# Q and K cast head by head in attention, and the DMA queue's order

## The chip, the cores and the metric

One core of a Trainium2 chip runs the whole program. The metric is the device time of one execution in microseconds (us). The kernel before took 928.75, 928.95 and 930.42 in three runs; the median is 928.95.

## The reference

Attention over 4 batches of 8 heads (576 positions, 64 wide), a mixture of experts with a capacity, and a dense layer behind it:

```
scores = q @ k.T / sqrt(D)                       # causal
cum    = cumsum(max(s, 0))
bias   = min(-(cum[:, None] - cum[None, :]), 0)
attn   = softmax(where(causal, -1e9, scores + bias)) @ v
x      = experts(attn)                           # token choice by gate, capacity N // E
out    = max(x @ w_in, 0) ** 2 @ w_out
```

The change touches the attention part and the conversion of w_out that runs beside it. Both kernels compute all of this.

## The kernel before

TensorE multiplies in fp32r, so each operand that must keep its precision is split: a rounded part (a cast to fp32r) and the rest (a subtraction). For a pair of heads the tiles are `Q1`, `K1`, `Q2` and `K2`. The raw loads `q2` and `k2` hold Q and K twice, in partitions 0 to 63 and 64 to 127. K1 is the cast of both copies of K; Q1 has the cast of Q in its lower half and Q's rest in its upper half; K2 holds K's rest and Q2 the cast of Q. One matmul of Q1 with K1 and one of Q2 with K2 (L205, L206) add up to the full product. Q2's 64 rows are copied from Q1 by a DMA (L174), and rows 64 to 67 of Q2 and K2 carry the bias: ones, and two rows from the cumulative sum that DMAs bring (L148, L149).

`attention` walks over 160 tiles, called steps here: 16 pairs of heads, ten steps a pair, five to a head. The five tiles of a head are its blocks of query rows, from the last (576 columns of scores) to the first (64). At a step, `scores` puts the matmuls of its tile on TensorE; `softmax` (L222, VectorE) takes the row maximum; then come the functions that the table `slot` holds for this step; `transposes` turns the tile of two steps before (L250, TensorE); `expo` (L233) is the exponent on ScalarE; and `flush` copies transposed tiles out of PSUM (L240 on VectorE, L238 on ScalarE). Values times weights (`av`, L276) run for the pair before, and `av_out` copies the result into oT.

The engines work through their instructions in the order in which the program issues them, so these tables set what stands behind what. `PR` and `P1` say at which step of a pair `prep` of the next pair is called: bias rows, K's cast (L162) and K's subtraction on GpSimd (L165) at step 2, Q's cast (L173), the DMA of Q2 and Q's subtraction (L175) at step 3, each over both heads (1152 columns). `load_pair` of the pair after next is called at the first step of a pair, ahead of its scores. `CS` places the conversion of w_out, one block of 512 columns a pair, sixteen in all: `load` (a DMA of 512 KB into r, L837) at step 2, `begin` at step 7 (ex on GpSimd, L850, and the first sg on VectorE, L874), `begin2` at step 8 (the second sg), `end` at step 9 (woutR, L885). In the first pair each comes five steps later (`C0`). What is not converted in attention is converted later, beside the experts, by `conv.step`.

All these DMAs are issued by SyncE, in order. Eight of its issues can be under way: an issue waits until the one eight before it has landed.

Of the kernel before, what the change touches and what calls it, by code (L numbers as in the profile page):

```python
# [7 lines left out]
FR = mybir.dt.float32r  # L8
# [3 lines left out]
AF = mybir.ActivationFunctionType  # L12
OP = mybir.AluOpType
# [3 lines left out]
B, H, S, D = 4, 8, 576, 64  # L17
# [5 lines left out]

XA = [1, 0]
LQ = 3
QP = 0
G2 = [(1, 5), (0, 1)]
G2L = [(3, 5), (0, 3)]
XB = 1
# [6 lines left out]
def f32(ap):  # L36
    return ap.bitcast(FT)
# [28 lines left out]
def attention(tc, cn, qT, kT, vm, vt, s, wg, xd, L):  # L66
    nc = tc.nc
    NP = B * H // 2
# [13 lines left out]
    wk = pool("a_wk", 2)  # L82
# [6 lines left out]
    RAW = {}  # L89
# [46 lines left out]
    nc.vector.tensor_sub(brow[:, 1, :], sr, f32(brow[:, 0, :]))  # L136
    PREP = {}

    def prep(p, u):
        if u == 0:  # L140
            q2, k2 = RAW[p]
            Q1 = wk.tile([128, 2, S], FR, name="Q1")
            K1 = wk.tile([128, 2, S], FR, name="K1")
            Q2, K2 = Q2S[p % 2], K2S[p % 2]
            PREP[p] = (Q1, K1, Q2, K2, q2)
            for a in range(2):
                hd = 2 * p + a
                nc.sync.dma_start(f32(K2[66:68, a, :]), f32(brow[hd:hd + 1]))  # L148
                nc.sync.dma_start(f32(Q2[64:66, a, :]), f32(brow[hd:hd + 1]))  # L149
            if p == 0:  # L150
                for a in range(2):
                    nc.scalar.activation(Q1[:, a], q2[:, a], AF.Copy)
                    nc.scalar.activation(Q2[0:64, a], q2[0:64, a], AF.Copy)
                    nc.vector.tensor_copy(K1[:, a], k2[:, a])
                    (nc.gpsimd if a else nc.vector).tensor_tensor(K2[0:64, a], k2[0:64, a], f32(K1[0:64, a]),
                                                                  op=OP.subtract)
                    nc.vector.tensor_tensor(Q1[64:128, a], q2[64:128, a], f32(Q1[64:128, a]), op=OP.subtract)  # L157
                return
            if QP:
                nc.gpsimd.tensor_tensor(Q1, q2, zero[:, :, None].to_broadcast([128, 2, S]), op=OP.add)  # L160
            if QP < 2:
                nc.vector.tensor_copy(K1, k2)  # L162
            else:
                nc.gpsimd.tensor_tensor(K1, k2, zero[:, :, None].to_broadcast([128, 2, S]), op=OP.add)
            nc.gpsimd.tensor_tensor(K2[0:64], k2[0:64], f32(K1[0:64]), op=OP.subtract)  # L165
        else:
            RAW.pop(p)
            if p == 0:
                ones(1)
                return  # L170
            Q1, K1, Q2, K2, qs = PREP[p]
            if not QP:
                nc.vector.tensor_copy(Q1, qs)  # L173
            nc.sync.dma_start(f32(Q2[0:64]), f32(Q1[0:64]))  # L174
            nc.gpsimd.tensor_tensor(Q1[64:128], qs[64:128], f32(Q1[64:128]), op=OP.subtract)  # L175


    E = [fx.tile([128, 128 * (i + 1)], FT, name=f"e{i}") for i in range(5)]
# [9 lines left out]
    tiles = [(hd, i) for hd in range(B * H) for i in (4, 3, 2, 1, 0)]  # L188

    def scores(hd, i):  # L190
        Q1, K1, Q2, K2 = PREP[hd // 2][:4]
        a = hd % 2
        n = max(256, NN[i])
        c0 = I0S[i]
        if i == 4:
            t = ps.tile([128, 2, 512], FT, name="sc4")
            parts = [(t[:, 0, :288], 0, 288), (t[:, 1, :288], 288, 576)]
            v = t[:, :, :288]
        else:
            t = ps.tile([128, 512], FT, name="sc", bufs=SCB)  # L200
            parts = [(t[:, :n], 0, n)]
            v = t[:IM[i], :NN[i]]
        for o, x0, x1 in parts:
            m = x0 <= c0 < x1
            nc.tensor.matmul(o, Q1[:, a, c0:c0 + 128], K1[:, a, x0:x1], start=True, stop=False)  # L205
            nc.tensor.matmul(o, Q2[:, a, c0:c0 + 128], K2[:, a, x0:x1], start=False, stop=not m)  # L206
            if m:
                nc.tensor.matmul(o[:, c0 - x0:c0 - x0 + IM[i]], cn.identb, cn.tri[:, :IM[i]], start=False, stop=True)  # L208
        SC[hd, i] = v
# [158 lines left out]
                f, a = jobs.popleft()  # L368
                f(*a)

    prep(0, 0)
    load_pair(1)
    load_v(0)

# [2 lines left out]
    for g in range(2):  # L377
        nc.sync.dma_start(wbd[64 * g:64 * g + 64, :, 8 * g:8 * g + 8],
                          bass.AP(tensor=wg.tensor, offset=wg.offset + g * 512, ap=[[8, 64], [1024, 4], [1, 8]]))
    prep(0, 1)  # L380
    slot = {}

    def at(t, f, *a):
        slot.setdefault(t, []).append((f, a))
# [1 line left out]
    NT = len(tiles)  # L386
    AVS = [0, 0, 4, 5, 5, 8, 8]
    ORD = 2
    P1 = 3
    C0 = 5  # L390
    LS_ = [2, 2, -1, -1, -1, -1, 0]
    LO_ = [3, 2]
    LT = 3
    GB = [12, 4]
    PTB = 3
    CS = [2, 7, 8, 9]
    PR = [2, 3]
    AVO = [1, 8]
    for p in range(NP):
        t0 = 10 * (p + 1) + LA  # L400
        last = p == NP - 1
        avs, avo = (LS_, LO_) if last else (AVS, AVO)
        for n in range(7):
            at(t0 + avs[n], av, p, n)
        at(t0 + avo[0], av_out, p, 0)
        at(t0 + avo[1], av_out, p, 1)
        if p + 1 < NP:
            at(10 * p + PR[0], prep, p + 1, 0)
            at(10 * p + (PR[1] if p else P1), prep, p + 1, 1)
        for f, n in zip((cn.conv.load, cn.conv.begin, cn.conv.begin2, cn.conv.end), CS):  # L410
            at(max(0, 10 * p + n + (0 if p else C0)), f, *([True] if f == cn.conv.begin else []))
# [14 lines left out]
    for t in range(tend):  # L426
        if t < NT:
            hd, i = tiles[t]
            if hd % 2 == 0 and i == 4:
                p = hd // 2  # L430
                if p + 2 < NP:
                    load_pair(p + 2)
# [381 lines left out]
class Convert:  # L814


    def __init__(self, tc, cn, win, wout):
        self.nc, self.cn = tc.nc, cn
        self.loaded = self.begun = self.done = 0
        self.hold = False  # L820
        self.two = set()
# [18 lines left out]
    def begin(self, pool=False):  # L840
        n = self.begun
        if n >= self.loaded:
            return
        self.begun += 1
        hw = self.r64[n][:, :, :, 1]
        ex = self.cn.cv.tile([128, 4, 128], FT, name="ex", bufs=3)
        sg = self.cn.cv.tile([128, 4, 128], I32, name="sg", bufs=1)

        if pool:
            self.nc.gpsimd.tensor_tensor(ex, hw.bitcast(FT), self.cn.m112[:, :, None].to_broadcast([128, 4, 128]),  # L850
                                         op=OP.mult)
        else:
            self.nc.scalar.activation(ex, hw.bitcast(FT), AF.Copy, scale=2.0 ** -112)
        if n < NB2:
            self.half(n, sg, 0, 13, OP.logical_shift_right)
        else:

            u = self.r64[n].rearrange("p c f w -> p (c f w)").bitcast(U16).rearrange("p (f w) -> p f w", w=4)
            o = sg.rearrange("p c f -> p (c f)").bitcast(U16).rearrange("p (f w) -> p f w", w=2)
            self.nc.scalar.activation(o[:, :, 0], u[:, :, 1], AF.Identity, bias=self.cn.mhalf, scale=2.0 ** -13)  # L860
        self.ex[n] = (ex, sg)

    def begin2(self):
        n = self.begun - 1
# [575 lines left out]
```

## Time and profile before

| what | us |
|---|---|
| median of three runs | 928.95 |
| the profiled execution | 930.37 |
| its span in the profile | 928.60 |
| TensorE busy | 879.3 (95%) |
| VectorE busy | 583.9 (63%) |
| ScalarE busy | 465.8 (50%) |
| GpSimd busy | 274.9 (30%) |

A profile is of one execution. Its times run from the start of the span. PE is TensorE, DVE VectorE, ACT ScalarE, POOL GpSimd and SP SyncE (SPq its queue). A number with L is a line of the kernel. Busy shares are over the whole span, while attention ends at about 223 us and the rest belongs to routing, experts and the dense layer; what a change in attention is worth is read from the rows of that stretch. Ends of matmuls are modelled, so starts are the safer reading.

### The profile page before, as it was taken

To read this page: it belongs to the slowest core of one execution; us is meant where nothing else is said; L and a number is where in the kernel's file an instruction comes from. 1 tells how busy PE (TensorE), PEld (TensorE's weight loads), DVE (VectorE), ACT (ScalarE), POOL (GpSimd) and SP (SyncE) were. 2 spreads that over 40 slices of the span, in tenths; PEclk is the share of its full clock that TensorE was granted. 3 is DMA by queue.
4 is the path that set the end of the run, shared out by engine and by line. 5 is a ranking of instruction groups with operands and counts; after the bars stand their busy time and mean duration, and the time that the engine had idled before them with its cause. 6 is when DMAs were issued, how large, how long until landed. Compare 5 with 4: busy or idle time off the path is not lost.

```text
span 928.6 us, 17302 instructions
## 1 busy us (share of the span) xinstructions
PE 879.3 (95%) x6200; PEld 736.5 (79%) x6200; DVE 583.9 (63%) x1565; ACT 465.8 (50%) x1092; POOL 274.9 (30%) x231
## 2 busy tenths in 40 slices
PE   4999999998788899999999999999999999999996
PEld 3676767766588877888998887989788899898885
DVE  7788988886787779847766556666633444442222
ACT  6677767776334666533543323453333454544332
POOL 4454554550103454625001000300100444523233
PEclk9999999999599999999999999999999999999998
DMA  6977597751635632304531100643100350140001
GB/s 168 226 192 188 141 245 190 189 150 46 203 96 156 198 103 88 91 1 142 165 104 37 33 1 12 212 125 96 35 1 1 93 168 1 53 119 1 0 1 46
DMA packets 73975, 95.60 MB, mean 103 GB/s; under 512 B 8128, under 2 KB 53184, under 8 KB 73888
## 3 DMA queue, kind: packets, MB, share of 16 engines
q1 hardware_dynamic: 68560, 79.93, 31.6%
q0 software_dynamic: 3360, 11.01, 3.7%
q10 hardware_dynamic: 1968, 3.54, 1.1%
q8 instruction: 49, 0.80, 0.3%
q14 instruction: 38, 0.31, 0.1%
HBM read 80.31 MB, written 9.44 MB: 97 GB/s over the span
## 4 chain that ended last, share of the span: by engine, by line
PE 79%; DVE 10%; DMA 4%; issue 3%; ACT 2%; POOL 1%; SPq 1%; DVEq 0%; ACTq 0%; POOLq 0%
PE h L1064 10%; PE h L1065 10%; PE h L1066 10%; PE acc L1112 7%; PE acc L1113 7%; PE acc L1114 7%; PE av L276 5%; PE pt L250 5%; PE acc L1064 3%; PE acc L1065 3%; PE acc L1066 3%; DVE Q L173 2%; DMA raw<-in_w 2%; PE sc L205 2%; PE sc L206 2%
## 5 line engine op out<-in xcount | busy, mean ns | idle before, releaser
L1174 ACT ACTIVATE s<-h 128x512 f32<-128x512 f32 (+1 forms) x80 | 44.4, 555 | 202.1 <-PE h L1066 173.2
L1178 DVE TENSOR_TENSOR s<-s 128x512 f32<-128x512 f32 (+1 forms) x80 | 51.1, 639 | 140.0 <-ACT sH L1177 139.9
L1064 PE MATMUL h<-yH,winH 128*128 128x512 f32 (+1 forms) x332 | 123.0, 371 | 0.7 <-ACT yH L1158 0.7
L1065 PE MATMUL h<-yL,winH 128*128 128x512 f32 (+1 forms) x332 | 120.6, 363 | 0.1
L1066 PE MATMUL h<-yH,winL 128*128 128x512 f32 (+1 forms) x332 | 120.3, 362 | 0.0
L1112 PE MATMUL acc<-wH,sH 128*128 128x512 f32 x288 | 114.8, 399 | 0.0
L989 ACT ACTIVATE wH<-raw 128x512 fp32r<-128x512 f32 x128 | 79.8, 628 | 68.5 <-DMA raw<-in_w 38.9
L1113 PE MATMUL acc<-wL,sH 128*128 128x512 f32 x288 | 112.4, 390 | 0.0
L1114 PE MATMUL acc<-wH,sL 128*128 128x512 f32 x288 | 112.4, 390 | 0.0
L233 ACT ACTIVATE e<-sc,nm 128x576 f32<-128x576 f32 (+4 forms) x160 | 84.0, 525 | 48.1 <-DVE junk L222 41.7
L1179 POOL TENSOR_TENSOR sL<-s,sH 128x512 fp32r<-128x512 f32 (+1 forms) x48 | 67.4, 1405 | 132.8 <-DVE s L1178 132.8
L992 DVE TENSOR_TENSOR wL<-raw,wH 128x512 fp32r<-128x512 f32 x104 | 74.6, 722 | 46.6 <-ACT wH L989 42.7
L222 DVE TENSOR_SCALAR_CACHE_REDUCE junk<-sc 128x576 bf16<-128x576 f32 (+4 forms) x160 | 77.7, 485 | 30.9 <-PE sc L208 20.5
L250 PE MATMUL pt<-ident,e 128*128 128x128 f32 x448 | 82.1, 289 | 7.5 <-ACT e L233 6.1
L205 PE MATMUL sc<-K,Q 128*128 128x288 f32 (+2 forms) x192 | 72.8, 384 | 10.4 <-DVE Q L157 10.4
L1064 PE MATMUL h<-xH,wH 128*128 128x288 f32 x256 | 78.5, 307 | 2.4 <-DVE hL L1142 2.0
L1064 PE MATMUL acc<-hH,wH 128*128 128x288 f32 x256 | 78.1, 305 | 1.7 <-ACT wH L989 1.7
L1066 PE MATMUL h<-xH,wL 128*128 128x288 f32 x256 | 76.0, 297 | 2.0 <-POOL wL L992 1.4
L1066 PE MATMUL acc<-hH,wL 128*128 128x288 f32 x256 | 76.1, 297 | 0.1
L1065 PE MATMUL h<-xL,wH 128*128 128x288 f32 x256 | 76.2, 297 | 0.0
L1065 PE MATMUL acc<-hL,wH 128*128 128x288 f32 x256 | 76.0, 297 | 0.0
L250 PEld LDWEIGHTS pt<-ident,e 128*128 128x128 f32 x448 | 49.4, 144 | 29.1 <-ACT e L233 19.1
(218 smaller groups left out, 2057.6 us busy)
## 6 DMA issues: line engine op xcount, KB each, us to landing
raw<-in_w SPq DMA_DIRECT2D x128, 256.0 KB
k<-in_kT SPq DMA_DIRECT2D x30, 288.0 KB
q<-in_qT SPq DMA_DIRECT2D x30, 288.0 KB
r<-in_wout SPq DMA_DIRECT2D x16, 512.0 KB
r<-in_win SPq DMA_DIRECT2D x16, 512.0 KB
vb<-in_vm SPq DMA_DIRECT2D x16, 256.0 KB
Q<-Q SPq DMA_DIRECT2D x8, 288.0 KB
QB<-Q SPq DMA_DIRECT2D x7, 288.0 KB
```

Source lines behind the costliest of these rows:

```text
L205: nc.tensor.matmul(o, Q1[:, a, c0:c0 + 128], K1[:, a, x0:x1], start=True, stop=False)
L222: nc.vector.tensor_scalar(o, v, -0.125, None, op0=OP.mult, op1=OP.min, accum_out=nm[:m])
L233: nc.scalar.activation(o, v, AF.Exp, bias=nm[:m], scale=0.125, accum_out=sums[b % 2][:m, i, hd % H:hd % H + 1])
L250: nc.tensor.transpose(pt[:, j, :], (E4[hd % 2] if i == 4 else E[i])[:, 128 * j:128 * j + 128], cn.ident)
L989: S.activation(hi, src, AF.Copy)
L992: (G if eng[1] == "G" else V).tensor_tensor(lo, src, f32(hi), op=OP.subtract)
L1064: T.matmul(o, wh, xh, start=first, stop=False)
L1065: T.matmul(o, wh, xl, start=False, stop=False)
L1066: T.matmul(o, wl, xh, start=False, stop=last)
L1112: T.matmul(o, hi[:, c0:c0 + 128], wh, start=f == 0, stop=False)
L1113: T.matmul(o, hi[:, c0:c0 + 128], wl, start=False, stop=False)
L1114: T.matmul(o, lo[:, c0:c0 + 128], wh, start=False, stop=f == NB2 - 1)
```

## The change

`prep` now works on one head, in two calls. The first casts Q's head (576 columns) on VectorE and issues the DMA of its Q2 rows; the second casts K's head on VectorE and puts both subtractions on GpSimd. Both calls of a head fall on one step: 4 for the first head and 9 for the second (in the first pair 5 and 9). A new function `bias` issues the bias rows, at step 1. `load_pair` of the pair after next moves from the start of the pair to step 5. The conversion of w_out gets a third part, `begin1`, with the first sg; `load` moves to step 9, `begin` stays at 7, `begin1` is at 8, `begin2` and `end` at 12 and 13, which is steps 2 and 3 of the next pair.

```diff
+    def bias(hd):
+        p, a = hd // 2, hd % 2
+        for t in (K2S[p % 2][66:68], Q2S[p % 2][64:66]):
+            nc.sync.dma_start(f32(t[:, a]), f32(brow[hd:hd + 1]))
...
-            nc.vector.tensor_copy(K1, k2)
-            nc.gpsimd.tensor_tensor(K2[0:64], k2[0:64], f32(K1[0:64]), op=OP.subtract)
+            nc.vector.tensor_copy(Q1, q)
+            nc.sync.dma_start(f32(Q2[0:64]), f32(Q1[0:64]))
         else:
-            nc.vector.tensor_copy(Q1, qs)
-            nc.sync.dma_start(f32(Q2[0:64]), f32(Q1[0:64]))
-            nc.gpsimd.tensor_tensor(Q1[64:128], qs[64:128], f32(Q1[64:128]), op=OP.subtract)
+            nc.vector.tensor_copy(K1, k)
+            nc.gpsimd.tensor_tensor(K2[0:64], k[0:64], f32(K1[0:64]), op=OP.subtract)
+            nc.gpsimd.tensor_tensor(Q1[64:128], q[64:128], f32(Q1[64:128]), op=OP.subtract)
...
-    P1 = 3
-    C0 = 5
+    CS0 = [7, 12, 13, 14, 15]
-    CS = [2, 7, 8, 9]
-    PR = [2, 3]
+    CS = [9, 7, 8, 12, 13]
+    PR = [4, 4, 9, 9]
+    PR0 = [5, 5, 9, 9]
...
+            for a in range(2):
+                at(10 * p + 1, bias, 2 * p + 2 + a)
+                for u in range(2):
+                    at(10 * p + (PR if p else PR0)[2 * a + u], prep, 2 * p + 2 + a, u)
+        if p + 2 < NP:
+            at(10 * p + 5, load_pair, p + 2)
...
+    def begin1(self):
+        n = self.begun - 1
+        if 0 <= n < NB2 and n not in self.one:
+            self.one.add(n)
+            self.half(n, self.ex[n][1], 0, 13, OP.logical_shift_right)
```

On TensorE the order of the instructions is the same in both kernels. On VectorE, in an even-numbered pair and the start of the next one, it was this (junk is the softmax, sg and woutR the conversion, eT and oT copies out of PSUM):

```order
L874 TENSOR_SCALAR sg<-r_616 128x512
L222 TENSOR_SCALAR junk,nm<-sc 64x64
L885 SCALAR_TENSOR_TENSOR woutR<-ex,sg 128x512
...
L222 TENSOR_SCALAR junk,nm<-sc 128x320
L162 CAST K_782<-k_562 128x1152
L222 TENSOR_SCALAR junk,nm<-sc 128x192
L240 COPY oT<-av 128x256
L173 CAST Q_781<-q_561 128x1152
L222 TENSOR_SCALAR junk,nm<-sc 64x64
```

and now it is this, from the end of one pair's second head on:

```order
L214 TENSOR_SCALAR junk,nm<-sc 64x64
L160 CAST Q_638<-q_489 128x576
L163 CAST K_639<-k_490 128x576
...
L214 TENSOR_SCALAR junk,nm<-sc 128x320
L877 TENSOR_SCALAR sg<-r_555 128x512
L214 TENSOR_SCALAR junk,nm<-sc 128x192
L232 COPY oT<-av 128x256
L888 SCALAR_TENSOR_TENSOR woutR<-ex,sg 128x512
L214 TENSOR_SCALAR junk,nm<-sc 64x64
L160 CAST Q_816<-q_661 128x576
L163 CAST K_817<-k_662 128x576
```

The long casts have left steps 2 and 3; casts of half the length follow the softmax of steps 4 and 9, and the end of the conversion has come to steps 2 and 3.

In SyncE's queue, at the start of the program behind the load of pair 1 (k_233, q_232), the order was as follows (K_190 and Q_188 from QB are bias rows, vb is V, wbd the gate's weights, r a block of w_out):

```order
L112 DMA vb_168<-in_vm 128x2x256
L113 DMA vb_168<-in_vt 64x2x64
L378 DMA wbd<-in_wg 64x4x8 x2
L99 DMA k_247<-in_kT 64x1152 x2
L99 DMA q_246<-in_qT 64x1152 x2
L148 DMA K_190<-QB 2x1x576
L149 DMA Q_188<-QB 2x1x576
L148 DMA K_190<-QB 2x1x576
L149 DMA Q_188<-QB 2x1x576
L174 DMA Q_188<-Q_274 64x1152
L837 DMA r_349<-in_wout 128x1024
```

and it is now:

```order
L141 DMA K_190<-QB 2x1x576
L141 DMA Q_188<-QB 2x1x576
L141 DMA K_190<-QB 2x1x576
L141 DMA Q_188<-QB 2x1x576
L161 DMA Q_188<-Q_315 64x576
L98 DMA k_323<-in_kT 64x1152 x2
L98 DMA q_322<-in_qT 64x1152 x2
L833 DMA r_349<-in_wout 128x1024
L161 DMA Q_188<-Q_315 64x576
```

The load of pair 2 has moved behind the bias rows and the first half of Q2, and the second half of Q2 stands behind that load and the block of w_out.

The last rows of VectorE's part in attention, with the two copies of the last transposed tiles, were and are:

```order
L885 SCALAR_TENSOR_TENSOR woutR<-ex,sg 128x512
L240 COPY eT_3063<-pt 128x2x128
L240 COPY eT_3063<-pt 128x64
L240 COPY oT<-sc 128x256
L289 TENSOR_SCALAR rinv<-sums_212 128x40
```

```order
L232 COPY eT_3129<-pt 128x64
L877 TENSOR_SCALAR sg<-r_2986 128x512
L888 SCALAR_TENSOR_TENSOR woutR<-ex,sg 128x512
L232 COPY oT<-sc 128x256
L281 TENSOR_SCALAR rinv<-sums_212 128x40
```

The last sg and woutR now stand between the copies of the transposed tiles and that of oT.

## Rows read from the trace of the kernel before

**Rows 1.** The chain that ended last: shares of the span by line

```profile
PE h L1064 10%; PE h L1065 10%; PE h L1066 10%; PE acc L1112 7%; PE acc L1113 7%; PE acc L1114 7%; PE av L276 5%; PE pt L250 5%; PE acc L1064 3%; PE acc L1065 3%; PE acc L1066 3%; DVE Q L173 2%; DMA raw<-in_w 2%; PE sc L205 2%; PE sc L206 2%
```

**Rows 2.** TensorE's waits, 40 to 205 us: us in total, times, longest

```profile
PE pt L250 <- ACT e L233: 2.0, 8, 0.3
PE pt L250 <- ACT eT L238: 1.4, 4, 0.4
PE sc L206 <- DMA Q<-Q: 0.3, 1, 0.3
```

**Rows 3.** TensorE's timeline, pair 2: start, us, engine, line, idle before it

```profile
39.15 0.38 PE L205 MATMUL sc<-K,Q 128*128 128x288 f32 x1
...
45.10 0.38 PE L205 MATMUL sc<-K,Q 128*128 128x288 f32 x1
...
47.62 0.33 PE L250 MATMUL pt<-ident,e 128*128 128x128 f32 x1 [0.25 <-ACT e L233]
...
51.40 0.38 PE L205 MATMUL sc<-K,Q 128*128 128x288 f32 x1
```

**Rows 4.** VectorE's timeline in pair 2

```profile
42.35 0.49 DVE L222 TENSOR_SCALAR_CACHE_REDUCE junk<-sc 128x320 bf16<-128x320 f32 x1
...
42.76 0.76 DVE L162 CAST K<-k 128x1152 fp32r<-128x1152 f32 x1
44.26 0.36 DVE L222 TENSOR_SCALAR_CACHE_REDUCE junk<-sc 128x192 bf16<-128x192 f32 x1 [0.74 <-PE sc L208]
...
44.88 2.05 DVE L173 CAST Q<-q 128x1152 fp32r<-128x1152 f32 x1
46.85 0.21 DVE L222 TENSOR_SCALAR_CACHE_REDUCE junk<-sc 64x64 bf16<-64x64 f32 x1
...
51.29 0.22 DVE L222 TENSOR_SCALAR_CACHE_REDUCE junk<-sc 64x64 bf16<-64x64 f32 x1
```

**Rows 5.** GpSimd's timeline in pair 2

```profile
43.65 2.66 POOL L165 TENSOR_TENSOR K<-k,K 64x1152 fp32r<-64x1152 f32 x1 [4.76 <-issue]
...
49.77 1.12 POOL L850 TENSOR_TENSOR ex<-r,m 128x512 f32<-128x512 f32 x1
```

**Rows 6.** Instructions of single lines: ns min/median/max, first and last start

```profile
L173 DVE CAST Q<-q x15: 739/2037/2094, 18.4 to 198.3; 128x1152 fp32r<-128x1152 f32 x15
...
L154 DVE CAST K<-k x2: 460/460/460, 8.3 to 10.4; 128x576 fp32r<-128x576 f32 x2
...
L155 POOL TENSOR_TENSOR K<-k,K x1: 1972/1972/1972, 10.9 to 10.9; 64x576 fp32r<-64x576 f32 x1
...
L874 DVE TENSOR_SCALAR sg<-r x32: 450/467/2007, 29.6 to 216.8; 128x512 uint16<-128x512 uint16 x32
```

**Rows 7.** TensorE's timeline at the start, steps 5 and 6

```profile
16.34 0.38 PE L205 MATMUL sc<-K,Q 128*128 128x288 f32 x1
...
20.76 0.33 PE L250 MATMUL pt<-ident,e 128*128 128x128 f32 x1 [2.21 <-ACT e L233]
```

**Rows 8.** VectorE's timeline at the start, steps 3 and 6

```profile
18.38 1.70 DVE L173 CAST Q<-q 128x1152 fp32r<-128x1152 f32 x1 [1.34 <-DMA q<-in_qT]
...
21.36 0.61 DVE L222 TENSOR_SCALAR_CACHE_REDUCE junk<-sc 128x448 bf16<-128x448 f32 x1
```

**Rows 9.** SyncE's issues at the start: loads of pairs 1 and 2, bias

```profile
10.75 1.17 SPq L99 DMA_DIRECT2D k<-in_kT  x2
...
17.30 1.53 SPq L99 DMA_DIRECT2D q<-in_qT  x2
19.59 0.64 SPq L148 DMA_DIRECT2D K<-QB  x1
```

**Rows 10.** One stretch: its length, busy us by engine, PEclk, DMA share, GB/s

```profile
16.00:40.00 24.00, 19.11 (x129) 14.20 (x129) 17.52 (x51) 14.86 (x48) 13.07 (x6) 0.93 1.00 235
```

**Rows 11.** VectorE: the last oT copy, and all woutR (busy, mean ns, idle)

```profile
222.32 0.42 DVE L240 COPY oT<-sc 128x256 f32<-128x256 f32 x1 [0.96 <-PE sc L276]
...
L885 DVE SCALAR_TENSOR_TENSOR woutR<-ex,sg 128x512 int32<-128x512 int32 x16 | 11.0, 685 | 0.0
```

More of the change, by code (lines that the diff above doesn't have):

```diff
@@ L25 @@
 LQ = 3
-QP = 0
 G2 = [(1, 5), (0, 1)]
@@ L137, in attention @@
     PREP = {}
-    def prep(p, u):
-        if u == 0:
[L141 to L149, printed above, removed]
-            if p == 0:
[L151 to L157, printed above, removed]
-                return
-            if QP:
-                nc.gpsimd.tensor_tensor(Q1, q2, zero[:, :, None].to_broadcast([128, 2, S]), op=OP.add)
-            if QP < 2:
-                nc.vector.tensor_copy(K1, k2)
-            else:
-                nc.gpsimd.tensor_tensor(K1, k2, zero[:, :, None].to_broadcast([128, 2, S]), op=OP.add)
-            nc.gpsimd.tensor_tensor(K2[0:64], k2[0:64], f32(K1[0:64]), op=OP.subtract)
-        else:
[L167 to L172, printed above, removed]
-                nc.vector.tensor_copy(Q1, qs)
-            nc.sync.dma_start(f32(Q2[0:64]), f32(Q1[0:64]))
-            nc.gpsimd.tensor_tensor(Q1[64:128], qs[64:128], f32(Q1[64:128]), op=OP.subtract)
@@ new lines, in bias, with prep @@
+    def bias(hd):
+        p, a = hd // 2, hd % 2
+        for t in (K2S[p % 2][66:68], Q2S[p % 2][64:66]):
+            nc.sync.dma_start(f32(t[:, a]), f32(brow[hd:hd + 1]))
+    def prep(hd, u):
+        p, a = hd // 2, hd % 2
+        q2, k2 = RAW[p]
+        if p not in PREP:
+            PREP[p] = (wk.tile([128, 2, S], FR, name="Q1"), wk.tile([128, 2, S], FR, name="K1"), Q2S[p % 2],
+                       K2S[p % 2])
+        Q1, K1, Q2, K2 = (t[:, a] for t in PREP[p])
+        q, k = q2[:, a], k2[:, a]
+        if u == 0:
+            if p == 0:
+                bias(hd)
+                nc.scalar.activation(Q1, q, AF.Copy)
+                nc.scalar.activation(Q2[0:64], q[0:64], AF.Copy)
+                nc.vector.tensor_copy(K1, k)
+                (nc.gpsimd if a else nc.vector).tensor_tensor(K2[0:64], k[0:64], f32(K1[0:64]), op=OP.subtract)
+                nc.vector.tensor_tensor(Q1[64:128], q[64:128], f32(Q1[64:128]), op=OP.subtract)
+                return
+            nc.vector.tensor_copy(Q1, q)
+            nc.sync.dma_start(f32(Q2[0:64]), f32(Q1[0:64]))
+        else:
+            nc.vector.tensor_copy(K1, k)
+            nc.gpsimd.tensor_tensor(K2[0:64], k[0:64], f32(K1[0:64]), op=OP.subtract)
+            nc.gpsimd.tensor_tensor(Q1[64:128], q[64:128], f32(Q1[64:128]), op=OP.subtract)
+            if a:
+                RAW.pop(p)
@@ L190, in scores @@
     def scores(hd, i):
-        Q1, K1, Q2, K2 = PREP[hd // 2][:4]
+        Q1, K1, Q2, K2 = PREP[hd // 2]
         a = hd % 2
@@ L369, in run_jobs @@
                 f(*a)
-    prep(0, 0)
+    for a in range(2):
+        prep(a, 0)
+    RAW.pop(0)
     load_pair(1)
@@ L379, in attention @@
                           bass.AP(tensor=wg.tensor, offset=wg.offset + g * 512, ap=[[8, 64], [1024, 4], [1, 8]]))
-    prep(0, 1)
+    ones(1)
     slot = {}
@@ L407, in attention @@
         if p + 1 < NP:
[L408 to L411, printed above, removed]
+            for a in range(2):
+                at(10 * p + 1, bias, 2 * p + 2 + a)
[3 more added lines that the diff above has]
+            at(10 * p + 5, load_pair, p + 2)
+        for f, n in zip((cn.conv.load, cn.conv.begin, cn.conv.begin1, cn.conv.begin2, cn.conv.end), CS if p else CS0):
+            at(10 * p + n, f, *([True] if f == cn.conv.begin else []))
         if p % 4 == 3:
@@ L430, in attention @@
                 p = hd // 2
-                if p + 2 < NP:
-                    load_pair(p + 2)
                 if p:
@@ L820, in __init__ @@
         self.hold = False
-        self.two = set()
+        self.one, self.two = set(), set()
         self.converted = []
@@ L854, in begin @@
         if n < NB2:
-            self.half(n, sg, 0, 13, OP.logical_shift_right)
+            if not pool:
+                self.half(n, sg, 0, 13, OP.logical_shift_right)
         else:
```

## The prediction

> **What bounds the kernel now.** I read the chain of waits first. Its longest lines are TensorE's matmuls, and among them stands one line of VectorE, the cast of Q at L173 with 2% of the span [rows 1]; so TensorE sets the pace, but one cast sits in its way. The change touches attention only (to 223 us), so I read TensorE's waits for pairs 2 to 15 next: twelve waits of a transpose for ScalarE, 3.4 us in sum, and one for a Q transfer [rows 2]. TensorE's timeline gives the size of one. I number the tiles as steps, ten to a pair of heads, five to a head; the 128x288 score matmul opens a head. Pair 2's head 0 opens at 39.15, head 1 at 45.10, pair 3 at 51.40 [rows 3]: 5.95 us for the five steps without a wait, 6.30 for the five with one. The wait is 0.25 us of idle before the transpose at 47.62, and about 0.1 more is late work, 0.35 together (I use 0.34). VectorE's timeline tells why: the Q cast starts at 44.88 and takes 2.05 us, and the softmax of step 4 waits behind it until 46.85 [rows 4]. The cast is long because GpSimd subtracts from 43.65 to 46.31 [rows 5]: over 15 casts it took 739 ns at best and 2037 at the median [rows 6].
>
> **The steady state.** A head's casts now are two of 128x576 at the end of a head (steps 4 and 9), Q then K, with both subtractions behind them. A cast of that form took 460 ns [rows 6], so 4 x 0.46 = 1.84 us a pair against 0.76 + 2.05 = 2.81. More than the sum counts where they lie. Between the softmax of step 2 (done at 42.84) and that of step 4 VectorE had K's cast, the softmax of step 3, the oT copy and the Q cast [rows 4]. In the new order this stretch holds one sg (0.47), the softmax, the copy and one woutR (0.69) [rows 6, 11]: from 44.26, when TensorE delivered step 3's scores, 0.36 + 0.08 + 0.42 + 0.69 gives a start of the small softmax at 45.8 instead of 46.85. Its exponent is then ready a microsecond earlier, and the transpose at 47.62, which needed 0.34, does not wait. What is late next is the 576-wide softmax behind the new casts: 45.8 + 0.28 + 0.92 = 47.0, against 46.85 + 0.28 = 47.1 at the earliest before, while TensorE comes 0.34 earlier; so it stands a little closer than it did. At step 9 the two casts take the place of one woutR (0.92 for 0.69), which had no wait behind it. I take the whole wait for twelve halves: 12 x 0.34 = -4.1 us; bounds -5.0 (thirteen, and every trace of lateness) and -1. The Q transfer's wait of 0.3 [rows 2] goes too: the halves are issued six steps, about 7 us, before use and no longer behind the big load in front of their pair.
>
> **GpSimd's queue** is the cover that can go. Its four subtractions of 64x576 are half of 2.65 us each, 1.33, plus 1.12 for one ex [rows 5]: 6.4 of 11.9 us a pair. They start when the casts of step 9 end, 51.51 + 0.92 by the row at 51.29 [rows 4], and end at 55.1. VectorE's next sg comes when the softmax of the next step 2 is done, 12.25 us after 42.84: at 55.1 too, so there is no margin before they meet. There is some before it matters: sg done at 43.31 (in pair 2's times) would wait for TensorE until 44.26, 0.95 us, and the small softmax has 0.7 more than the 0.34 it must win. Only 1.6 us of lateness bring the old wait back. The row of the one 64x576 subtraction in the trace shows 1972 ns, not 1330: VectorE worked beside it [rows 6]. The Trainium skill, page "SBUF — State Buffer", section "Who interferes with whom", has a rule that speaks against the change: the first of the two engines to issue holds the shared ports for the whole instruction and the other fully blocks. The trace agrees as far as the 2037 beside the 739 goes. By that rule each subtraction could be held by a whole VectorE instruction, and the sg behind it by a whole subtraction; carried through, it gives the time of the slower rival below, while the margin of 1.6 us from the rows leaves the sum as it is.
>
> **The start.** Before, K's cast of pair 1 stood at step 2 and Q's at step 3, and Q's waited 1.34 us for its load [rows 8]; TensorE's transpose at step 6 waited 2.21 [rows 7]. Steps 5 to 20 took 39.15 - 16.34 = 22.8 us, against 3 x 5.95 = 17.9 without waits: at most 5 to win. Now both casts stand at step 5, behind a softmax that is done at about 18.0; Q's load still lands at 18.35, so casts end at 19.3 and the softmax of step 6 starts near 19.7 rather than 21.36, 1.6 us earlier. But transfers get later. SP's fourth bias row takes the place at which the last load of pair 2 was issued, 18.35 [rows 9], and the next issue stood until V had landed, at 19.59 [rows 9]; there now stands Q's first half, then the load of pair 2 at 20.2 (it was issued before and around 17.30), w_out's block at 22.6, Q's second half at 23.2. The load of pair 1 took from 10.75 to 18.35 for 1.18 MB: 5.0 us at 235 GB/s [rows 10] and 2.6 around it. So pair 2 lands at 20.2 + 7.6 = 27.8, the block of 0.52 MB 2.2 us later at 30.0, the second half of Q at 30.6. Two things wait for these: head 1 of pair 1 (step 15), which would be ready at about 28, until 30.6; and VectorE's sg, now at step 13 in front of step 14's softmax, until 30.0. Behind it come sg, two casts and a 576-wide softmax, 0.5 + 0.3 + 0.5 + 0.9 + 0.8, to 33, and a woutR beside a subtraction. I make step 20 start at 38.0, against 39.15: -1.2 us. Bounds: -4.1 if the two transfers land before they are asked for, +1.5 if TensorE idles through and its clock falls longer (granted 0.93 from 16 to 40 [rows 10]).
>
> **The end of attention and later.** The last conversion's sg and woutR move in front of the last oT copy. VectorE idles 0.96 until 222.32 [rows 11]; from 221.36 on, 0.47 + 0.69 end at 222.5, so the copy is 0.2 late: +0.2, bounds 0 and +1.2. One conversion of w_out, of sixteen, no longer fits (pair 1's begin finds nothing loaded, as the load now comes two steps behind it) and moves into the experts' stage with 2 x 0.47 + 0.69 = 1.6 us of VectorE [rows 6, 11], one step later for each that follows. TensorE rarely waits there and VectorE has room, so 0; bounds -1 and +1.6. Two early loads of w_in at the end of attention also go; the conversions that need them start some 80 us on.
>
> **Sum.** -4.1 - 0.3 - 1.2 + 0.2 = -5.4 us. The profiled execution took 930.37 (span 928.60 and 1.77 around it), so 925.0 on its scale; it is 1.42 above the median of the three runs, 928.95, on which I forecast 923.5. The likeliest case's own range is 921 to 926.5.
>
> **Rivals.**
> (a) The start gives all it can: the transfers land in time, steps 5 to 20 take 18.7 us. Then -4.1 instead of -1.2: 920.6. For it: the DMA engines are the ones that are full there, and less is queued in front of head 0's Q. Against: the load of pair 2 is issued 4 us later.
> (b) The wait does not go but changes its name: the 576-wide softmax behind the casts, or the copies behind it, stops TensorE in its place. Then the steady term falls to -1 and the start to 0: about 928. For it: it stands closer than before. Against: steps 8 and 9 held an sg and a woutR of 0.69 and no wait stands behind them [rows 2, 3].
> (c) Slower, by GpSimd. The change would then not do what it says, since VectorE meets GpSimd as before, only in sg instead of the cast. If the second Q half's subtraction ends more than 1.6 us late, the sg at step 2 takes the 2007 ns of the worst row [rows 6] or more, and one at step 8 likewise behind ex. A VectorE instruction of 2.0 us in such a place costs 0.34 today, once a pair; twice a pair it costs 0.68, thirteen times 0.34 more than now: +4.4, with the start at +1.5 and +0.2 at the end about 935; with one such place the steady term is 0 and the start decides, 928 to 931. It decides from subtractions of about 2.1 us each; the longest seen is 1.97.
>
> **Chances.** The forecast 0.63, (a) 0.13, (b) 0.14, (c) 0.10. Within 0.2% (1.9 us) is about what a measurement can tell from no change. Of the forecast and (a) nearly all is faster; of (b) half is, at most; so faster 0.80, same 0.11, slower 0.09. The range reaches from (a)'s lower part to (b): 918.5 to 928.5.
>
> **What would show it.** In the new profile: TensorE opens a head every 5.95 us in pairs 2 to 14, both halves; the waits for e and eT are gone; Q's casts take about 0.46, none near 2.0; the subtractions 1.3 to 1.4. At the start: pair 2's casts and head 1's second matmul at step 15 wait for transfers that land between 27 and 31, VectorE's first sg too; step 20 opens near 38. At the end: the last oT copy near 0.2 us later against the last matmul in front of it. I am wrong if sg instructions of 1 to 2 us appear at steps 2 and 8 in most pairs, if a new wait of 0.3 follows the casts, or if step 20 opens later than 39.

## The result, and the profile after

| | kernel before | changed kernel |
|---|---|---|
| median of seven runs each, us | 929.63 (928.75 to 932.41) | 921.45 (920.42 to 925.89) |
| profiled execution; its span | 930.37; 928.60 | 920.64; 918.6 |
| TensorE busy | 879.3 | 875.4 |
| VectorE busy | 583.9 | 565.9 |

The ratio is 0.9915, with a 95% interval of 0.9899 to 0.9931: 8 us faster, where 5.4 were forecast. Ratios here and below count fast executions alone; of the ten with the moved subtraction one took 2403.77 us, which its median counts and its ratio does not. The two profiled executions differ by 9.7 us, because the one of before lay 0.7 above its median and the one of after 0.8 below.

Where the time went is read best from the start of each head, that is of its first 128x288 score matmul. In TensorE's timeline of the changed kernel pair 2 reads as follows, and the last head opens at 203.62:

```profile
36.46 0.38 PE L197 MATMUL sc<-K,Q 128*128 128x288 f32 x1
...
42.41 0.38 PE L197 MATMUL sc<-K,Q 128*128 128x288 f32 x1
...
48.40 0.38 PE L197 MATMUL sc<-K,Q 128*128 128x288 f32 x1
...
203.62 0.38 PE L197 MATMUL sc<-K,Q 128*128 128x288 f32 x1
```

The same head in the kernel before:

```profile
211.39 0.38 PE L205 MATMUL sc<-K,Q 128*128 128x288 f32 x1
```

Step 20 opens 2.69 us earlier than in [rows 3], step 155 opens 7.77 earlier, so 5.08 came in between. A second head takes 5.99 us here against 6.30. Not every head is that short: from step 55 on most of them take 6.0 to 6.8 us, since other work stands between their scores; they are compared with the same heads of the kernel before. TensorE has no wait left in the stretch in which [rows 2] had three lines; the windows view (length, busy us of PE, PEld, DVE, ACT, POOL, clock, DMA share, GB/s) has it busy throughout:

```profile
40.00:205.00 165.00, 165.00 (x1313) 119.76 (x1309) 128.33 (x453) 128.56 (x394) 88.09 (x67) 1.00 0.71 191
```

VectorE's timeline over the second head of pair 2 and the first of pair 3 answers to [rows 4]: no cast near 2 us, and all of them behind the small softmax.

```profile
48.44 0.45 DVE L160 CAST Q<-q 128x576 fp32r<-128x576 f32 x1
48.81 0.45 DVE L163 CAST K<-k 128x576 fp32r<-128x576 f32 x1
...
52.02 0.60 DVE L877 TENSOR_SCALAR sg<-r 128x512 uint16<-128x512 uint16 x1
...
54.31 0.68 DVE L888 SCALAR_TENSOR_TENSOR woutR<-ex,sg 128x512 int32<-128x512 int32 x1
```

GpSimd's timeline beside it answers to [rows 5]. The subtraction of 50.89 ends at 52.29; the sg of 52.02 met it and lost 0.13 us.

```profile
49.40 1.41 POOL L164 TENSOR_TENSOR K<-k,K 64x576 fp32r<-64x576 f32 x1 [1.95 <-PE sc L200]
50.89 1.40 POOL L165 TENSOR_TENSOR Q<-q,Q 64x576 fp32r<-64x576 f32 x1
```

By line (ns min/median/max), Q's cast answers to the first row of [rows 6]; it never met a subtraction:

```profile
L160 DVE CAST Q<-q x30: 395/447/460, 18.6 to 197.6; 128x576 fp32r<-128x576 f32 x30
```

At the start the transfers landed about a microsecond before the forecast. VectorE waited for the block of w_out until 28.72 and its conversion then met GpSimd twice; TensorE waited until 29.77 for the second half of Q, which this matmul reads (the row names V's transfer, the next in the queue):

```profile
19.69 0.61 DVE L214 TENSOR_SCALAR_CACHE_REDUCE junk<-sc 128x448 bf16<-128x448 f32 x1
...
28.72 0.46 DVE L877 TENSOR_SCALAR sg<-r 128x512 uint16<-128x512 uint16 x1 [0.56 <-DMA r<-in_wout]
...
29.21 1.16 DVE L877 TENSOR_SCALAR sg<-r 128x512 uint16<-128x512 uint16 x1
...
31.67 1.51 DVE L888 SCALAR_TENSOR_TENSOR woutR<-ex,sg 128x512 int32<-128x512 int32 x1
```

```profile
28.30 0.38 PE L197 MATMUL sc<-K,Q 128*128 128x288 f32 x1
...
29.77 0.37 PE L198 MATMUL sc<-K,Q 68*128 68x288 f32 x1 [1.09 <-DMA vb<-in_vm]
```

The end, answering to [rows 11]:

```profile
214.69 0.42 DVE L232 COPY oT<-sc 128x256 f32<-128x256 f32 x1
```

It is 7.63 earlier, so 0.14 later against step 155. From this copy to the end of the span it is 703.9 us, 706.3 before. All thirteen profiled executions, before, after and the eleven experiments below, lie between 703.0 and 706.6 there, though most of them do the same work; these 2.4 us are within that spread.

### The profile page after: what moved, and what is told of

Read it like the earlier page. It is cut to its first block, busy times and chain, and to the rows that moved or that the text cites. A ratio compares the mean times of both kernels' runs of the same rounds, so it can differ in the third digit from the quotient of the medians.

```text
span 918.6 us, 17406 instructions
## 1 busy us (share of the span) xinstructions
PE 875.4 (95%) x6200; PEld 735.1 (80%) x6200; DVE 565.9 (62%) x1595; ACT 468.6 (51%) x1093; POOL 278.5 (30%) x260
## 4 chain that ended last, share of the span: by engine, by line
PE 85%; DVE 4%; DMA 2%; issue 2%; POOL 1%; ACT 1%; SPq 0%; POOLq 0%; DVEq 0%; ACTq 0%
PE h L1067 11%; PE h L1069 10%; PE h L1068 10%; PE acc L1115 7%; PE acc L1116 7%; PE acc L1117 7%; PE pt L242 6%; PE av L268 6%; PE acc L1067 3%; PE acc L1068 3%; PE acc L1069 3%; PE sc L197 3%; PE sc L198 3%; PE mi L680 2%; PE mi L1034 1%
## 5 line engine op out<-in xcount | busy, mean ns | idle before, releaser
L1069 PEld LDWEIGHTS h<-yH,winL 128*128 128x128 f32 x332 | 62.5, 188 | 10.7
```

The costliest lines, as they stand in the source:

```text
L1069: T.matmul(o, wl, xh, start=False, stop=last)
```

## The experiments

The theory: the gain in the steady state comes from casts that no longer meet GpSimd's subtractions. Rivals: the place of the load or of the conversion did it, or the start alone. Each diff is against the kernel that its paragraph names. Lengths of heads are differences of their opening matmuls.

**The load back at the pair's start.** Changed kernel:

```diff
-        if p + 2 < NP:
-            at(10 * p + 5, load_pair, p + 2)
...
             if hd % 2 == 0 and i == 4:
                 p = hd // 2
+                if p + 2 < NP:
+                    load_pair(p + 2)
```

> The changed kernel with one part undone: the load of the pair after next is issued at the start of a pair again, ahead of bias rows and Q halves. Theory (the load's place matters at the start only): heads open every 5.95 to 5.99 us in pairs 2 to 14 as in the changed kernel; at the start Q's first half lands behind the load of pair 2, at about 26 instead of before 22.9, so step 10 waits about 3 us, the block of w_out is there earlier, and step 20 opens at 37.5 to 39 (36.46 in the changed kernel): 1 to 2.5 us slower than it. Rival (the place of the load is what frees the Q transfers in every pair): waits for Q halves of 0.2 to 0.5 us in most pairs, 4 us or more slower.

Measured: 930.66 median, ratio to before 1.0012 (0.9988 to 1.0037): the whole gain is gone. TensorE's waits of 40 to 205 us, and two lines of SyncE's (us in total, times, longest):

```profile
PE sc L198 <- DMA Q<-Q: 7.5, 6, 2.0
```

```profile
SPq L98 <- POOL K L164: 7.2, 11, 0.7
...
SPq L98 <- POOL Q L165: 3.1, 12, 0.3
```

The two raw buffers come free only when the subtractions behind step 9 have run. In SyncE's timeline the load that is called as a pair opens at 50.11 is issued at 52.54 and 54.03, as GpSimd's subtractions end (52.51 and 54.00), and Q's first half follows behind V and the bias rows at 60.59:

```profile
52.54 1.15 SPq L98 DMA_DIRECT2D k<-in_kT  x2
54.03 1.10 SPq L98 DMA_DIRECT2D q<-in_qT  x2
...
60.59 0.53 SPq L161 DMA_DIRECT2D QB<-Q  x1
```

The rival holds, with fewer and longer waits than it named (six, up to 2.0 us); of the theory only step 20 came true, which opens at 38.19. So the late casts need the later load. (This profiled run took 935.75, above its median.)

**The load at step 5, in the kernel before.**

```diff
+        if p + 2 < NP:
+            at(10 * p + 5, load_pair, p + 2)
...
-                if p + 2 < NP:
-                    load_pair(p + 2)
```

> The kernel before with one thing of the change alone: the large load of Q and K at step 5 of the pair instead of its start. Theory (the load's place matters only where the raw buffers come free late, which is so after the casts are split by heads, not in the kernel before): the heads of the kernel before within 0.05 us, the time within 1.5 us of it. Rival (a load at the pair's start delays the smaller transfers behind it in SyncE's queue, whatever the casts do): the wait for Q's transfer in the kernel before (0.3 to 0.5 us at one head of four pairs) goes, the time falls by 1.5 us or more.

Measured: 930.21, ratio 0.9994 (0.9979 to 1.0009), no change. Neither side is wholly right. Second heads of 6.3 stay at 6.28 to 6.30; but the first head of pair 9, which waited for Q's transfer, takes 6.41 instead of 6.91, as the rival said. The second head of pair 6 is 0.36 longer, so that from step 20 to step 155 the run is only 0.2 us shorter. And the start loses: the second head of pair 1 takes 10.02 instead of 7.12. There an sg met the subtraction and took 2.55 us, but it took 2.01 in the kernel before too, so this is a part of the loss only; the rest was not traced. The last oT copy is 2.15 later than before, and the rest of this execution 1.7 shorter, within the spread named above.

**The subtraction issued behind Q's cast, in the kernel before.** K's subtraction moves in the program from behind K's cast to behind Q's.

```diff
-            nc.gpsimd.tensor_tensor(K2[0:64], k2[0:64], f32(K1[0:64]), op=OP.subtract)
...
             nc.sync.dma_start(f32(Q2[0:64]), f32(Q1[0:64]))
+            nc.gpsimd.tensor_tensor(K2[0:64], k2[0:64], f32(K1[0:64]), op=OP.subtract)
```

> The kernel before with one line moved: GpSimd's subtraction for K is issued behind Q's cast, not behind K's; casts stay whole pairs at steps 2 and 3, loads and conversion stay. Theory (what cost 0.34 us a pair was the cast of Q held by GpSimd, not its length or place): Q's cast takes 0.76 us in all pairs, the waits of 0.2 to 0.4 us at step 6 are gone, second heads take 5.97 instead of 6.30 us, and attention is 4 to 5 us shorter from step 20 on; with 0.5 to 1 at the start the time is 924 to 925. Rival (two casts of a whole pair in steps 2 and 3 are too much there, so halving and moving them is what pays): at least half of the waits stay and the gain is 2 us or less.

Measured: 931.29, ratio 1.0003 (0.9991 to 1.0016). The edit moved nothing, so it decides nothing: the subtraction still started at 43.73, since GpSimd was free and waited for K's cast alone.

```profile
43.73 2.64 POOL L174 TENSOR_TENSOR K<-k,K 64x1152 fp32r<-64x1152 f32 x1 [4.79 <-issue]
```

The order of the program counts within one engine; to part the two, the casts themselves must change places.

**Q's cast first, in the kernel before.** For whole pairs, with load and conversion as before:

```diff
-            nc.vector.tensor_copy(K1, k2)
-            nc.gpsimd.tensor_tensor(K2[0:64], k2[0:64], f32(K1[0:64]), op=OP.subtract)
+            nc.vector.tensor_copy(Q1, q2)
+            nc.sync.dma_start(f32(Q2[0:64]), f32(Q1[0:64]))
         else:
...
-            nc.vector.tensor_copy(Q1, qs)
-            nc.sync.dma_start(f32(Q2[0:64]), f32(Q1[0:64]))
+            nc.vector.tensor_copy(K1, ks)
+            nc.gpsimd.tensor_tensor(K2[0:64], ks[0:64], f32(K1[0:64]), op=OP.subtract)
             nc.gpsimd.tensor_tensor(Q1[64:128], qs[64:128], f32(Q1[64:128]), op=OP.subtract)
```

> The kernel before with one thing of the change alone: in each head Q's cast and the transfer of its second half stand a step ahead of K's cast, so that GpSimd's two subtractions run behind both casts; the load, the start and the conversion of the output weights stay where they were. Theory (the casts met GpSimd's subtractions, and TensorE waited for that at six steps of each pair): Q's cast of second heads falls from 2.0 to about 0.76 us or less, the waits at the head openings and for Q's second half between 40 and 205 us go from some 3.4 us (2.0 and 1.4) to under 0.8, a second head takes 5.97 instead of 6.27 to 6.32 us, and the time falls by 3 to 5 us to 925 to 928 us. Rival (the length of the pair is set by the place of the load and of the conversion, not by the casts): more than half of the waits stay, the time is within 1.5 us of the kernel before. Both may be mixed: the conversion's two parts at steps 7 to 9 now stand next to the subtractions; each that meets one takes up to 2 us instead of 0.46 or 0.68, which can bring back 0.1 to 0.3 us of waits per pair.

Measured: 934.55, ratio 1.0039 (1.0023 to 1.0056): slower. The cause was treated as expected: Q's cast took 756 ns at the median, and four of the five second heads that had taken 6.3 us took 6.06. But first heads of 5.96 went to 6.71. VectorE's, GpSimd's and TensorE's timelines at the end of pair 3 and the start of pair 4:

```profile
62.80 2.74 DVE L870 TENSOR_SCALAR sg<-r 128x512 uint16<-128x512 uint16 x1 [0.44 <-DMA r<-in_wout]
65.44 0.33 DVE L218 TENSOR_SCALAR_CACHE_REDUCE junk<-sc 128x192 bf16<-128x192 f32 x1
```

```profile
62.60 2.63 POOL L171 TENSOR_TENSOR Q<-q,Q 64x1152 fp32r<-64x1152 f32 x1
```

```profile
65.28 0.40 PE L201 MATMUL sc<-K,Q 128*128 128x288 f32 x1 [0.20 <-POOL Q L171]
```

The sg now meets the subtraction that the cast has avoided, and the softmax stands behind it. The subtraction ends at 65.23, and the pair's opening matmul waits 0.20 us for it.

**The same, with the conversion out of the way.**

```diff
-    CS = [2, 7, 8, 9]
+    CS = [7, 11, 12, 14]
```

> The kernel before with Q's cast and transfer a step ahead of K's cast (GpSimd's two subtractions behind both, whole pairs as in the kernel before), and with the conversion of the output weights moved to where GpSimd doesn't subtract: load at step 7, sign parts at steps 1 and 2 of the next pair, the rest at its step 4; 15 conversions in the attention. Theory (a subtraction costs something only where a VectorE instruction on two SBUF operands meets it late; in the run with Q's cast first alone it was the sign part at step 8 that took 2.1 us and cost 0.75 us per first head): first heads go back to 5.96 us, second heads to at most 6.06, the time is 923 to 926 us, 9 to 11 us below that run. Rival (two whole-pair subtractions, 5.3 us in one piece, don't fit whatever the conversion does: the split by heads is what makes room): first heads stay over 6.4 us, the time is over 930 us.

Measured: 940.91, ratio 1.0104 (1.0075 to 1.0134). My theory's forecast fell, and the time is the rival's, but neither has the heads: first heads of 6.71 went to 6.31, not to 5.96 and not over 6.4. The opening matmul now waits for GpSimd in five pairs (PE, then POOL):

```profile
66.29 0.40 PE L201 MATMUL sc<-K,Q 128*128 128x288 f32 x1 [0.29 <-POOL Q L171]
```

```profile
60.44 3.11 POOL L170 TENSOR_TENSOR K<-k,K 64x1152 fp32r<-64x1152 f32 x1 [5.92 <-PE pt L250]
63.62 2.62 POOL L171 TENSOR_TENSOR Q<-q,Q 64x1152 fp32r<-64x1152 f32 x1
```

From K's cast on, two whole-pair subtractions take 5.8 us, a whole head: second heads take 6.5, first heads 6.3. And the conversion was not out of the way everywhere. In three pairs a woutR still met K's subtraction and took 2.73 us:

```profile
86.57 2.73 DVE L881 SCALAR_TENSOR_TENSOR woutR<-ex,sg 128x512 int32<-128x512 int32 x1
```

These three second heads take 9.90, 8.63 and 8.62 us, where the kernel before has 7.2: 5.5 us more in sum, by the theory's own mechanism. Taken off, some 935 us would be left by this estimate, still over the kernel before. So whole-pair subtractions did not fit here, though more than half of the loss is these three meetings; why first heads took 6.3 was not traced. In the changed kernel the two that end at 52.29 are wanted at 54.35, where the next head opens: the split by heads leaves 2.1 us of room.

**K's subtraction twice, in the changed kernel.** The second writes the same values again.

```diff
             nc.gpsimd.tensor_tensor(K2[0:64], k[0:64], f32(K1[0:64]), op=OP.subtract)
+            nc.gpsimd.tensor_tensor(K2[0:64], k[0:64], f32(K1[0:64]), op=OP.subtract)
```

> The changed kernel, in which GpSimd's subtraction for K is issued twice in each head (the second writes the same values again), so that GpSimd's pair of subtractions ends some 1.4 us later. Theory (VectorE has 1.6 us to spare at steps 2 and 8, and a conversion part that meets a subtraction only uses this up): the conversion parts at steps 2 and 8 take 1 to 2 us instead of 0.47 to 0.60, TensorE's waits between 40 and 205 us stay below 1 us in all, and the time is within 1.5 us of the changed kernel's. Rival (the slower case of the prediction: the delayed conversion part delays the casts and with them the next head): about 0.3 us of waits per pair, some 4 us of waits between 40 and 205 us, and a time 3 to 8 us over the changed kernel's.

Measured: 926.24, ratio to before 0.9954 (0.9936 to 0.9972), about 4 us over the changed kernel. From step 20 to step 155 it is 3.2 us longer, by 0.16 to 0.48 in eight first heads, though TensorE's waits there sum to 0.5 us. So the rival is right in kind: 1.5 us of delay are already too much. The mechanism is not the sg alone. VectorE, and below it GpSimd:

```profile
61.36 0.76 DVE L878 TENSOR_SCALAR sg<-r 128x512 uint16<-128x512 uint16 x1
...
62.15 1.16 DVE L160 CAST Q<-q 128x576 fp32r<-128x576 f32 x1
```

```profile
60.40 1.40 POOL L166 TENSOR_TENSOR Q<-q,Q 64x576 fp32r<-64x576 f32 x1
61.87 1.12 POOL L847 TENSOR_TENSOR ex<-r,m 128x512 f32<-128x512 f32 x1
```

GpSimd's delay pushes ex from behind step 8 into Q's cast. The heads speak for this: where Q's cast starts late and takes 1.16 us they are 0.43 to 0.48 longer, while three heads in which the sg of step 2 took 1.14 to 1.17 us too, but Q's cast started in time and took 1.00 to 1.02, are 0.04 to 0.08 longer.

**K's cast a step earlier, in the changed kernel.** Q's cast then meets K's subtraction, as before.

```diff
-    PR = [4, 4, 9, 9]
+    PR = [3, 4, 8, 9]
...
-            nc.vector.tensor_copy(Q1, q)
-            nc.sync.dma_start(f32(Q2[0:64]), f32(Q1[0:64]))
-        else:
             nc.vector.tensor_copy(K1, k)
             nc.gpsimd.tensor_tensor(K2[0:64], k[0:64], f32(K1[0:64]), op=OP.subtract)
+        else:
+            nc.vector.tensor_copy(Q1, q)
+            nc.sync.dma_start(f32(Q2[0:64]), f32(Q1[0:64]))
```

> The changed kernel, in which K's cast (and GpSimd's subtraction behind it) is moved one step ahead of Q's cast after the first pair, so that Q's cast meets the running subtraction, as in the kernel before; load, conversion and bias rows stay as in the changed kernel. Theory (the meeting is what cost the kernel before its waits): Q's cast takes 1.2 to 2.0 us instead of 0.46, TensorE waits 0.1 to 0.6 us per head between 40 and 205 us, 3 to 15 us in all, and the time is 3 to 15 us over the changed kernel's. Rival (the meeting costs VectorE time that it has to spare, and the gain came from the load's place and the conversion's): Q's cast grows, but the waits stay under 1 us in all and the time is within 1.5 us of the changed kernel's.

Measured: 929.05, ratio 0.9974 (0.9955 to 0.9994), 5.5 us over the changed kernel by the ratios; 6.1 of them lie between steps 20 and 155. The theory holds, and the loss goes with the length of the meeting. In nine first heads Q's cast takes 1.53 to 1.54 us and the head is 0.34 to 0.62 longer (6.30 instead of 5.96 in five, the length of the kernel before's second heads); in three second heads it takes 1.27 to 1.28 and they are 0.66 to 0.69 longer; in four first heads it takes 0.94 to 0.97 and nothing is lost. By line:

```profile
L163 DVE CAST Q<-q x30: 436/952/1540, 18.9 to 204.1; 128x576 fp32r<-128x576 f32 x30
```

**The conversion's steps as before, in the changed kernel.**

```diff
-    CS0 = [7, 12, 13, 14, 15]
+    CS0 = [7, 12, 12, 13, 14]
-    CS = [9, 7, 8, 12, 13]
+    CS = [2, 7, 7, 8, 9]
```

> The changed kernel with the steps of the output weights' conversion as in the kernel before (sign parts at steps 7 and 8, the rest at step 9, 16 conversions in the attention), casts, load and bias rows as changed. Theory (a margin of about 1.6 us in VectorE): sign and rest parts that meet the subtractions take 1 to 2 us, and TensorE waits at most 0.1 us per pair, so the time is within 2 us of the changed kernel's. Rival (the conversion's place had to move with the casts): the delayed parts push back the casts at step 9 and the next head opens late, 0.2 to 0.5 us per pair, 3 to 7 us over the changed kernel's.

Measured: 924.3, ratio 0.9936 (0.9916 to 0.9956). Step 155 is 1.5 us late: the first head of pair 2 takes 6.48 once, three heads take 0.27 more and one 0.10; the rest are as in the changed kernel, second heads too, in most of which an sg takes 0.8 to 1.3 us. That is nearer to the theory, but the interval does not part a loss of 2 us from none.

**The bias rows with Q's cast, in the changed kernel.**

```diff
-                at(10 * p + 1, bias, 2 * p + 2 + a)
+                at(10 * p + (PR if p else PR0)[2 * a], bias, 2 * p + 2 + a)
```

> The changed kernel with the bias rows issued right ahead of each transfer of Q's second half instead of at step 1. Theory (SyncE's queue has room: two issues of some 0.6 us each ahead of a transfer that is due several steps later): heads within 0.02 us of the changed kernel's, the time within 1 us of it. Rival (the rows' place in the queue is part of the gain): Q's second half lands later by 1 to 1.5 us, TensorE waits for it in some heads, 0.2 us or more per pair, 3 us or more in all.

Measured: 920.51, ratio 0.9898 (0.9881 to 0.9915); from step 20 on all heads are within 0.02 us, though step 20 itself opens 0.6 later. The rows' place is worth nothing that these runs can show, as the theory had it.

**A block of w_out more in the first pair.** Changed kernel, with sixteen conversions beside attention instead of fifteen:

```diff
+        if not p:
+            at(9, cn.conv.load)
```

> The changed kernel with one more load of w_out at step 9 of the first pair, so that sixteen blocks are converted in attention as before, not fifteen. Theory (the 2.4 us that the profiles differ by behind attention come from the clock's falls in routing, not from the moved conversion): from the last oT copy to the end it takes 703 to 706 us, and differs from the changed kernel by less than its own runs do; in attention up to 1 us more at the start for 0.5 MB more, so 921 to 923. Rival (a lighter start of the experts' conversions is worth 1 to 2.4 us): behind the last oT copy it takes 706 us or more, 923 to 924 in all.

Measured: 922.08, ratio 0.991 (0.9887 to 0.9932). Step 20 opens 1.05 later; from the last oT copy on it takes 703.8 us, as in the changed kernel: the conversion that moved to the experts' stage costs nothing that these runs can show.

**The first conversion later.** In the first pair of the changed kernel only the load remains, behind Q's second half:

```diff
-    CS0 = [7, 12, 13, 14, 15]
+    CS0 = [9, 12, 13, 14, 15]
...
-            at(10 * p + n, f, *([True] if f == cn.conv.begin else []))
+            if p or f == cn.conv.load:
+                at(10 * p + n, f, *([True] if f == cn.conv.begin else []))
```

> The changed kernel with the first pair's conversion cut to its load, at step 9 behind the second half of Q; the first block is converted at steps 17 to 23, which found nothing loaded before, so there are fifteen conversions in attention as in the changed kernel. Theory (steps 15 to 20 took 8.2 us there because Q's second half queues behind the block of w_out and because VectorE stands for that block in sg and then meets GpSimd in woutR): second half landed by 28.3, step 15's wait under 0.3 us, steps 15 to 20 in 6.0 to 6.3 us, step 20 at 34.3 to 34.8 instead of 36.46, so 1.7 to 2.2 us faster than the changed kernel. Rival (the loads of pairs 1 and 2 bound the start and the block only comes on top): VectorE's casts at step 14 wait for the load of pair 2 until 29 or later, and step 20 opens at 36 or later, within 0.6 us of the changed kernel.

Measured: 919.22, ratio 0.9878 (0.986 to 0.9897): faster than both kernels. The theory holds: the second head of pair 1 no longer waits and takes 5.97 instead of 8.16, and step 20 opens 1.86 before the changed kernel's:

```profile
28.63 0.38 PE L197 MATMUL sc<-K,Q 128*128 128x288 f32 x1
...
34.60 0.38 PE L197 MATMUL sc<-K,Q 128*128 128x288 f32 x1
```

## Why the prediction was right, and where it was not

**The steady state** (forecast -4.4 with the Q transfer, measured -5.08). The mechanism is shown: put back the meeting of Q's cast and K's subtraction, and the heads of 6.30 come back, in first heads this time, and only where the meeting is long. The count and size were a little short: thirteen second heads from step 25 on are shorter, by 0.13 to 0.47 and 4.65 in sum, where I took twelve by 0.34; the Q transfer's wait gave 0.50 at one head where I took the 0.3 of [rows 2]. There the wait view shows the idle time alone, and the head opening shows the late work behind it as well. That a head opens every 5.95 us was forecast for all of pairs 2 to 14; it does so only where no other work stands in the head.

**GpSimd's margin** (forecast 1.6 us). The sg of step 2 did meet the subtraction, but by 0.13 us, and nothing came of it. Subtractions of 1.40, not 1.33, took 0.14 us of the margin a head. One subtraction more, 1.5 us, cost some 3 us; with the 0.14 that is just the 1.6, so the size is not disproved. The way was another: I had worked it out for sg and the small softmax, and left out that ex, behind the subtractions in GpSimd's queue, then reaches Q's cast.

**The start** (forecast -1.2, measured -2.69 at step 20). This is the mis-sized term: of the 2.2 us by which the last oT copy came earlier than forecast, 1.5 are here. Casts and softmax fell where forecast (step 6's softmax at 19.69, forecast 19.7), and step 15 opened at 28.30 (forecast about 28). Landing was set too late: the block of w_out came at 28.72 (forecast 30.0) and Q's second half at 29.77 (forecast 30.6); step 20 opened 1.5 us before the forecast's 38.0. The load of pair 2, ahead of both, was issued at 19.74 (forecast 20.2). The rate that I had assumed, the 235 GB/s of [rows 10], was not what was off: from 19.74 to 28.72 the windows view shows 240 GB/s. What is left, some 0.8 us by this reckoning, is in the 2.6 us that I had put around the load; which part of them did not recur was not tried. That the block's place held step 20 is shown: without this conversion step 20 opens at 34.60. But that run takes away two things at once, Q's second half behind the block and VectorE's sg and woutR behind it, and does not part them.

**The end** (forecast +0.2): +0.14. **Later** (forecast 0): -2.4 between the two profiled executions, within the spread of others; the sixteenth conversion made no difference.

**The rivals.** (a) came half true, by 1.5 of its 2.9 us. (b) did not come. (c) did not come. One subtraction more a head brings a part of its loss, by way of ex and Q's cast and not by sg; what it describes, VectorE meeting GpSimd in sg instead of the cast, is what happened with Q's cast first for whole pairs.

**The parts together.** None of the parts that were tried alone gains: the load alone 0.9994, the exchanged casts alone 1.0039, the change without its load 1.0012. Late casts free the raw buffers late, so the load must move; both subtractions behind both casts need a head's length for a whole pair, and split by heads they fit. The split alone and the conversion's new steps alone were not tried in the kernel before; in the changed kernel the conversion's steps are worth some 2 us or nothing.

## What to carry to other kernels

When two engines slow each other, moving one of them needs the time at which its result and its buffers are wanted: list for each moved instruction what it will meet next, who waits for its end, and which transfer waits for the buffer that it frees. Judge such an edit by the distance between fixed points of the bound engine's work, here the openings of the heads; the list of waits shows only part of it. At the start of a program, where transfers are queued closely, leave out what nobody needs yet.

## What the runs showed of the hardware

A VectorE instruction that started beside a running GpSimd instruction ended a fixed time behind its end. For the sg it was 0.31 to 0.34 us in all 178 meetings in the first 230 us of the thirteen traces in which it started 0.14 us or more before that end: the sg of 52.02 ends 0.33 behind 52.29, the one of 62.80 ends 0.31 behind 65.23. The 576-wide Q cast did the same in 30 of 31 (the cast of 62.15 in the doubled run ends 0.32 behind 62.99); in the other, GpSimd was itself held by the sg ahead of the cast, and the cast went first. Alone both take 0.45 to 0.46, so all but 0.14 of the work was done after GpSimd let go. The 1152-wide Q cast ended 0.62 behind in 42 meetings, 14 of them in the kernel before [rows 4, 5], and woutR 0.55 in 25. Softmaxes and copies, which read PSUM, took no longer beside a GpSimd instruction (0.76 us for the 576-wide softmax of the kernel before, both ways). The Trainium skill, page "SBUF — State Buffer", section "Who interferes with whom", says that the first of the two holds the shared ports for its whole instruction and the other fully blocks; these ends agree with it.

The granted clock differed at the start. From 22.2 to 25.6 us it was 0.51, the lower of the clock's two levels (1.2 GHz of 2.4), in the kernel before, which had idled 2.21 us ahead of it [rows 7], and 1.00 in the changed kernel, whose single waits there were about 1 us or less; 18 matmuls fitted in the one and 24 in the other. So step 10, which opens 2.9 us earlier in the changed kernel (22.72 instead of 25.62), gains by the clock as well as by the earlier casts; the runs do not part the two. The windows view of before, then of after:

```profile
22.20:25.60 3.40, 3.40 (x18) 3.03 (x18) 1.02 (x6) 2.65 (x9) 0.63 (x1) 0.51 0.99 219
```

```profile
22.20:25.60 3.40, 3.14 (x24) 2.21 (x23) 2.92 (x13) 2.84 (x10) 2.08 (x3) 1.00 1.04 239
```
